# Five edits to the order of work in an attention and feed-forward kernel: a bank pair exchanged, a sum and an add issued in earlier steps, eight bias matmuls in place of five unread ones, one load ahead of another, values behind two products

## The chip, the cores and the metric

The kernel runs on one core of a Trainium2 chip. The core has five engines that run side by side, each through its own instructions in order: TensorE (matmuls; PE in the profile, and PEld for its weight loads), VectorE (DVE), ScalarE (ACT), GpSimd (POOL) and SyncE (SP). They wait for one another through semaphores. POOL and SP here issue most of the transfers (DMA) between the core's memory and the chip's main memory. TensorE writes only into PSUM, an accumulator memory of eight banks; VectorE and ScalarE read results out of them.

The metric is the device time of one execution, in microseconds (us), lower is better. All times below are in us unless they are marked ns, and positions are counted from the start of the profiled span.

## The reference

```python
scores = (q @ k^T) / sqrt(64)                          # 8 batches, 8 heads, 576 tokens
mask = (rel >= 0) & (rel < 128)                        # rel = query position - key position
attn = softmax(where(mask, scores - slope[h] * |rel|, -1e9))
x = (attn @ v), heads side by side                     # 4608 tokens x 512
h = x @ w_in                                           # 512 x 2048
g = where(h > 0, h, exp(min(h, 0)) - 1)
out = g @ w_out                                        # 2048 x 512, float32
```

Each query looks at itself and at the 127 keys before it, with a bias that falls linearly with the distance at a slope of its head.

## The kernel before, in words

**Attention.** A batch `b` has 576 tokens, in five blocks of 128 (the last has 64). For each block `u` of keys, scores are formed for the queries that can see it, ScalarE takes exponentials (`early_expo`, `first_expo`, `expo`) into `EX[u]`, and VectorE multiplies them with a table of bias and mask (`first_weigh`, `weigh`, L216 and L241). Batch 0 adds bias and mask on TensorE instead: matmuls with scaled identities (`early_bias`, L183, and `bias`, L166) write into the bank, and scores are added to them (`early_scores`, L191, and `first_scores`, L176). `values` (L253, a quarter of the banks) and `all_values` (L271, all heads into the bank pair `spa`, batches 2 to 7) then multiply with v, and a column of ones gives the softmax's denominator: VectorE takes a reciprocal and multiplies with it (L259 and L260, or L276 and L277). The result `xn` is turned into `xT` by `turn`: on TensorE with a copy (batches 0 and 1) or by a transfer that SP's queue issues (L285).

**Loads of q, k and v** are issued by POOL. Batches 0 and 1 come in pieces (`load_first`, L101), which TensorE transposes (`turn_first`, L136); later ones come by `load_qk` (L108) and VectorE turns them (`turn_qk`, L145). `load_v` is L114.

**Feed-forward.** `hidden` (L305) multiplies `xT` with w_in into `hp[0]`, `hp[1]` (some early blocks into others), ScalarE and POOL or ScalarE alone prepare the exponential, and `elu` (VectorE, L323) writes `g`. For most tokens the product with w_out isn't made directly but in the form with seven products of half size for a pair of 128-token blocks: pair `n` takes four sums of `g` blocks on VectorE (`sums`, S1 to S4, L354), seven products of eight matmuls each (`product`, L393), and adds that put the output together (`combine`: C11, C12, C22, also L354). Only the first two blocks of 128 tokens use the direct form (`output`, L329). Products of a pair go into two banks, `z` and `x`, chosen by the table `XY`: products 1, 6, 7 and 4 into `z`, products 2, 5 and 3 into `x`. ScalarE copies products 1, 6, 7 and 5 out (`kept`, L396). C11 adds the copy of product 1 to product 2, which lies in `x`; product 5 is the next to overwrite `x`.

**The order of work** is written by hand. After a start-up part (to L495) the loop at L674 goes through numbered steps `s`. In a step, these are emitted one after the other: `early` entries, the step's `hidden`, the `elu` of the step before, the `tasks` (entries by `at`, and by `at_once`, which puts them first), the `OUT` list (seven single product matmuls in most steps), and the `late` entries (by `after`). An engine runs its share in just this order, so an entry's place decides what stands ahead of it in each queue.

The steps concerned: the start-up has `warm(5, sp[0])` (L492), matmuls that nobody reads. Step 1 forms the second half of block 1's scores in `AB`, which is `spa`. In steps 11 and 12 POOL issues the third pieces of batch 1's k and q, in step 17 they are transposed. Steps 18 to 23 have no `hidden`; they begin batch 1's attention and the first pair (n = 1, steps 19 to 30). Before, its products 1, 6, 7, 4 go to `op` and 2, 5, 3 to `sp[3]`; the direct output of step 18 uses `op` too. `all_values(b, u)` comes in step `START[b] + 4 * u + 3`.

Of the kernel before, what the change touches and what calls it, by code (L numbers as in the profile page):

```python
# [18 lines left out]
def kernel(  # L19
# [57 lines left out]
    sp = [spa[:, 0, :], spa[:, 1, :]] + [ps_s.tile([128, 512], F32, name=f"sp{i}", tag=f"sp{i}") for i in (2, 3)]  # L77
    hp = [ps_h.tile([128, 512], F32, name=f"hp{i}", tag=f"hp{i}") for i in range(2)]
    av = ps_v.tile([128, 512], F32, name="av", tag="av")
    op = ps_o.tile([128, 512], F32, name="op", tag="op")  # L80
    AB = sp[0:2]
# [67 lines left out]
    with tc.manual_schedule():  # L149
# [29 lines left out]
        def early_bias(banks, c0):  # L179

            for x in range(4):
                for hh in range(2):
                    nc.tensor.matmul(banks[hh][:, 128 * x:128 * x + 128], SI[:, 4 * hh + x, :], RB[:, c0:c0 + 128],  # L183
                                     start=x == 0, stop=False, skip_group_check=True)
# [58 lines left out]
        def values(b, i, part, bank=av):  # L243

            m = 128 if i < 4 else 64
            banks = (part, part + 2) if b < 2 else (2 * part, 2 * part + 1)
            parts = [(3, 128, 3), (3, 192, 4)] if i == 4 else [(i, 0, i)] + ([(i - 1, 128, i - 1)] if i else [])
            a = bank[:, 0:4 * (D + 1)].rearrange("p (x h d) -> p x h d", x=2, h=2)
            for x, g in enumerate(banks):
                for h2 in range(2):  # L250
                    for j, (u, c, n) in enumerate(parts):
                        c += 512 * g + 256 * h2
                        nc.tensor.matmul(a[:, x, h2, :], ex_[u][:, c:c + 128], VP[b % 2][:, n, 2 * g + h2, 0:D + 1],  # L253
                                         start=j == 0, stop=j == len(parts) - 1)
            if part == 0:
                xnt[b, i] = work.tile([128, 4, 2, D], F16, name="xn", tag="xn", bufs=4)
            o = xnt[b, i][0:m, part::2, :, :] if b < 2 else xnt[b, i][0:m, 2 * part:2 * part + 2, :, :]
            r = work.tile([128, 2, 2], F32, name="rden", tag="rden", bufs=2)
            V.reciprocal(out=r[0:m], in_=a[0:m, :, :, D])  # L259
            V.tensor_tensor(out=o, in0=a[0:m, :, :, 0:D], in1=r[0:m].unsqueeze(3).broadcast_to([m, 2, 2, D]),  # L260
                            op=ALU.mult)
# [18 lines left out]
        def turn(b, i, copy=None, bank=op):  # L280
            n = 128 if i < 4 else 64
            o = (b * S + 128 * i) % RING
            x = xnt.pop((b, i)).rearrange("p g h d -> p (g h d)")
            if copy is None:
                nc.sync.dma_start_transpose(out=xT[:, :, o:o + n], in_=x[0:n, :])  # L285
                return
            t = bank.bitcast(F16)[:, 0:512].rearrange("p (c r) -> p c r", c=4)
            for c in range(4):
                nc.tensor.transpose(t[:, c, 0:n], x[0:n, 128 * c:128 * c + 128], ident[0:n, 0:n])
            copy(xT[:, :, o:o + n], t[:, :, 0:n])  # L290
# [80 lines left out]
        def place(n, i):  # L371


            z, x = XY[n] if n < 2 * NTB - 1 else (sp[2], sp[3] if i == 2 else sp[0])
            return (z if i in (1, 4, 6, 7) else x)[:, 0:256]
# [53 lines left out]
        def warm(n, bank=op):  # L429
            for _ in range(n):  # L430
                nc.tensor.matmul(bank[:, 0:256], wz[:, 0:128], wz, start=True, stop=True)
# [57 lines left out]
        early_expo((hp[1], av), 1, 0)  # L489
        values(0, 0, 0, hp[0])  # L490
        values(0, 0, 1, op)
        warm(5, sp[0])  # L492
        turn(0, 0, V.tensor_copy, hp[0])
        values(0, 1, 0)
        values(0, 1, 1, op)  # L495


        early, tasks, late, HID, OUT = {}, {}, {}, {}, {}

        def at(s, f, *a):  # L500
            tasks.setdefault(s, []).append((f, a))

        def at_once(s, f, *a):
            tasks.setdefault(s, []).insert(0, (f, a))

        def after(s, f, *a):
            late.setdefault(s, []).append((f, a))

        def before(s, f, *a):
            early.setdefault(s, []).append((f, a))  # L510
# [14 lines left out]
                HID[16 * t + 6 + j] = [(t, *step, BUF[(j + 1) % 2])]  # L525
        SEVEN = range(1, 18)

        XY = {1: (op, sp[3]), 2: (op, av)}
        for n in range(3, 2 * NTB):
            XY[n] = XY[n - 1][::-1]  # L530
        for o in range(16 * NTB):
            t, ts, f = o // 16, o // 4 % 4, o % 4
            if o // 8 in SEVEN:
                continue
            s = (9, 11, 13, 14)[o] if o < 4 else 11 + o if o < 13 else 2 * o - 1 if o < 16 else 15 + o
            OUT[s] = [(output, (t, ts, 4 * f, op if ts else sp[0]))]

        def done(r):
            for step in HID[r]:
                elu(*step)  # L540
# [2 lines left out]
        at(0, turn, 0, 1, V.tensor_copy)  # L543
        at(0, turn_first, 0, 0, 1, 0, sp[3], nc.scalar.copy)
        before(1, done, 0)
        at(1, early_bias, AB, 128)
        at(1, early_scores, AB, 1, 128)
        at(1, early_expo, AB, 1, 128)
        at(1, turn_first, 0, 1, 1, 0, av, V.tensor_copy)
# [28 lines left out]
        at(5, load_first, 1, 1, 0)  # L578
        at(9, load_first, 1, 0, 0)
        at(11, load_first, 1, 1, 1)  # L580
        at(12, load_first, 1, 0, 1)
        for n, s in enumerate((10, 11, 13, 14, 15)):
            at(s, load_v, 1, n)
        at(16, turn_first, 1, 1, 0, 0, av, V.tensor_copy)
# [5 lines left out]
        for u, a in ((0, 18), (1, 20)):  # L590
            for half in range(2):
                after(a, first_scores, 1, u, half, 2 * half)
                after(a, first_expo, 1, u, half, 2 * half, 0, 256)
                at(a + 1 + half, first_weigh, 1, u, half)
                if (u, half) != (1, 0):
                    after(a + 2 + half, values, 1, u, half, av if half else sp[2])
        after(22, turn, 1, 0, nc.scalar.copy, av)
# [19 lines left out]
        for b in range(2, B):  # L617
            for u in range(4):
                a = START[b] + 4 * u
                after(a, scores, b, u)  # L620
                for g in range(4):
                    before(a + 1 + g // 2, expo, b, u, g)
                at(a + 1, weigh, b, u, 0)
                at(a + 2, weigh, b, u, 1)
                at(a + 3, all_values, b, u)
                at(a + 3, turn, b, u)
                if u == 3:
                    at(a + 4, values, b, 4, 0, sp[2])
                    at(a + 4, values, b, 4, 1, sp[3])
                    at(a + 4, turn, b, 4)  # L630
            a = START[b - 1] if b > 2 else 0
            for n in range(4):
                piece = (b, int(n < 2), n % 2)
                if b == 2:
                    m = 4 if n < 2 else 6
                    at(TURN[b][n], turn_qk, *piece, 0, m)
                    at(REST[n], turn_qk, *piece, m, R)
                else:
                    at(TURN[b][n] if b == 3 else a + 4 * n, turn_qk, *piece)
            for n in range(8):  # L640
                at(a - 8 + n if a else 16 + n // 2, load_qk, b, int(n < 4), n % 4)
            for n in range(5):
                at(a + 3 + n if a else 20 + n // 2, load_v, b, n)
# [5 lines left out]
        for n in SEVEN:  # L649
            s = 15 + 8 * n  # L650
            ps = (19, 20, 21, 22, 23, 25, 27, 29, 30) if n == 1 else range(s, s + 9)
            if n < 2 * NTB - 1:
                for d, i in ((-1, 1), (1, 2), (3, 3), (4, 4)):
                    (at_once if n > 2 or n == 1 and i == 2 else at)(ps[d] if d > 0 else ps[0] - 1, sums, n, i)
                after(ps[2], combine, n, "C11")
                after(ps[6], combine, n, "C12")
                (at_once if n > 2 else at)(ps[8], combine, n, "C22")
                for d in range(8):
                    OUT[ps[d]] = [(product, (n, i, j, j + 1)) for i, j in turns[7 * d:7 * d + 7]]
            else:  # L660
                at_once(s - 3, sums, n, 3)
                for i in (2, 1):
                    at_once(s - 2, sums, n, i, 0, 6)
                    at_once(s - 1, sums, n, i, 6, 8)
                at(s - 1, product, n, 1)
                OUT[s] = [(product, (n, 2)), (combine, (n, "C11")), (sums, (n, 4)), (product, (n, 6)), (product, (n, 5))]
                OUT[s + 1] = [(product, (n, 7)), (product, (n, 3)), (combine, (n, "C22")), (combine, (n, "C12")),
                              (last_out, (n,))]
# [5 lines left out]
        for s in range(min(slots), max(slots) + 1):  # L674
            for f, a in early.get(s, []):
                f(*a)
            for step in HID.get(s, []):
                hidden(*step, s in SOFT)
            if s - 1 in HID and s not in (1, 4, 5):
                done(s - 1)  # L680
            for f, a in tasks.get(s, []):
                f(*a)
            for f, a in OUT.get(s, []):
                f(*a)
            for f, a in late.get(s, []):
                f(*a)
# [30 lines left out]
```

## Time and profile before

| | |
|---|---|
| median of 3 runs | 309.42 (308.7 to 309.49) |
| the profiled execution | 309.05 |
| its span, first to last instruction | 307.2 |
| TensorE clock granted | 1.0 |
| TensorE / VectorE / ScalarE / POOL busy | 97% / 84% / 79% / 35% of the span |
| matmuls of `hidden` (L305) | 144.2 busy |
| loads through POOL's queue | 18.36 MB |

A line of a timeline gives start, duration, engine, line, operation, what is written and read, sizes and count; brackets hold idle time of the engine just before it and what ended that. A line of waits gives who waited for whom: total, times, longest. The chain goes back from the last instruction, at each step to what released it. Names come without buffer numbers (`sp` for `sp[2]` and `sp[3]`, `s` for the staging of q and k in batches 0 and 1, `st` for later ones). Idle time of an engine that nobody waits for costs nothing.

### The profile page before, as it was taken

To read this page: it belongs to the slowest core of one execution; us is meant where nothing else is said; L and a number is where in the kernel's file an instruction comes from. 1 tells how busy PE (TensorE), PEld (TensorE's weight loads), DVE (VectorE), ACT (ScalarE), POOL (GpSimd) and SP (SyncE) were. 2 spreads that over 40 slices of the span, in tenths; PEclk is the share of its full clock that TensorE was granted. 3 is DMA by queue.
4 is the path that set the end of the run, shared out by engine and by line. 5 is a ranking of instruction groups with operands and counts; after the bars stand their busy time and mean duration, and the time that the engine had idled before them with its cause. 6 is when DMAs were issued, how large, how long until landed. Compare 5 with 4: busy or idle time off the path is not lost.

```text
span 307.2 us, 9841 instructions
## 1 busy us (share of the span) xinstructions
PE 299.3 (97%) x4079; PEld 256.6 (84%) x4079; DVE 257.6 (84%) x499; ACT 241.5 (79%) x445; POOL 108.8 (35%) x163
## 2 busy tenths in 40 slices
PE   7999998999999999999999999999999999999996
PEld 5788875898888888988888888888899888888885
DVE  5647878988989999997989998989998788886783
ACT  5576787769797798878888889778988797968881
POOL 8947848572343224141615061706000001010000
PEclk9999999999999999999999999999999999999999
DMA  9999999999395919294959995999730302230103
GB/s 97 174 200 199 202 183 193 113 123 110 33 154 74 170 27 170 37 163 42 134 68 139 111 106 76 138 127 116 64 97 3 95 17 88 19 97 1 73 16 121
DMA packets 96941, 32.04 MB, mean 104 GB/s; under 512 B 83968, under 2 KB 92800, under 8 KB 96896
## 3 DMA queue, kind: packets, MB, share of 16 engines
q0 software_dynamic: 75920, 18.36, 65.2%
q1 hardware_dynamic: 20832, 12.98, 18.2%
q8 instruction: 32, 0.52, 0.7%
q14 instruction: 13, 0.11, 0.1%
q10 hardware_dynamic: 144, 0.07, 0.1%
HBM read 36.70 MB, written 9.44 MB: 150 GB/s over the span
## 4 chain that ended last, share of the span: by engine, by line
PE 77%; DMA 6%; ACT 5%; DVE 5%; POOL 3%; issue 2%; POOLq 0%; DVEq 0%; ACTq 0%
PE hp L305 35%; PE op L393 13%; PE av L393 13%; PE spa L225 4%; DMA s<-in_q_dram 3%; PE spa L271 3%; DMA wi<-in_moe_w_in_dram 2%; PE sp L393 2%; DVE g L323 2%; ACT e L315 2%; PE sp L253 1%; ACT EX L236 1%; POOL e L316 1%; POOL VP L114 1%; PE sp L305 1%
## 5 line engine op out<-in xcount | busy, mean ns | idle before, releaser
L305 PE MATMUL hp<-xT,wi 128*128 128x256 f16 (+3 forms) x1488 | 144.2, 245 | 1.0 <-DVE g L323 0.5
L305 PEld LDWEIGHTS <-wi 128*128 128x128 f16 x1600 | 119.7, 98 | 18.2 <-issue 5.8
L323 DVE SCALAR_TENSOR_TENSOR g<-e,hp 128x512 f16<-128x512 f32 x138 | 93.6, 679 | 22.4 <-ACT e L313 12.7
L316 POOL TENSOR_SCALAR e<-e 128x512 f32<-128x512 f32 x44 | 28.4, 645 | 154.6 <-ACT e L315 151.3
L312 ACT ACTIVATE e<-hp 128x512 f32<-128x512 f32 x98 | 58.6, 598 | 28.8 <-PE hp L305 23.2
L313 ACT ACTIVATE e<-e 128x512 f32<-128x512 f32 x100 | 63.1, 631 | 3.2
L393 PEld LDWEIGHTS <-S 128*128 128x128 f16 x544 | 51.4, 98 | 7.5 <-issue 1.8
L393 PEld LDWEIGHTS <-g 128*128 128x128 f16 x400 | 37.5, 98 | 4.5 <-issue 0.4
L241 DVE TENSOR_TENSOR EX<-EX,TAB 128x1024 f16<-128x1024 f16 x48 | 32.9, 686 | 6.1 <-ACT EX L236 4.0
L114 POOL DMA_DIRECT2D VP<-in_v_dram x40 | 34.3, 867 | 3.0 <-DMA s<-in_k_dram 1.8
L315 ACT ACTIVATE e<-hp 128x512 f32<-128x512 f32 x40 | 24.0, 601 | 10.6 <-PE hp L305 10.6
L393 PE MATMUL op<-T,S 128*128 128x256 f16 x200 | 30.0, 273 | 0.0
L233 ACT ACTIVATE EX<-spa 128x1024 f16<-128x1024 f32 x24 | 24.6, 1026 | 3.7 <-PE spa L225 3.4
L393 PE MATMUL av<-T,S 128*128 128x256 f16 x176 | 26.4, 272 | 0.1
L236 ACT ACTIVATE EX<-sp 128x512 f16<-128x512 f32 x48 | 26.0, 597 | 0.0
L354 DVE TENSOR_TENSOR S<-g 128x1024 f16<-128x1024 f16 (+2 forms) x35 | 23.5, 671 | 0.7 <-PE op L393 0.2
L393 PE MATMUL op<-wo,g 128*128 128x256 f16 x128 | 19.0, 272 | 0.1
L393 PE MATMUL av<-wo,g 128*128 128x256 f16 x120 | 18.0, 273 | 0.0
L108 POOL DMA_DIRECT2D st<-in_k_dram x24 | 16.3, 688 | 3.1 <-DMA s<-in_q_dram 1.9
L277 DVE TENSOR_TENSOR xn<-spa,rden 128x512 f16<-128x512 f32 x24 | 16.6, 692 | 0.8
L108 POOL DMA_DIRECT2D st<-in_q_dram x24 | 15.9, 668 | 0.6 <-DMA VP<-in_v_dram 0.4
L271 PE MATMUL spa<-VP,EX 128*128 128x65 f16 x336 | 15.5, 193 | 0.1
(139 smaller groups left out, 380.3 us busy)
## 6 DMA issues: line engine op xcount, KB each, us to landing
out_dram<-ob SPq DMA_DIRECT2D x32, 256.0 KB, 3.1
VP<-in_v_dram POOLq DMA_DIRECT2D x32, 128.0 KB, 6.0
st<-in_k_dram POOLq DMA_DIRECT2D x24, 144.0 KB, 5.6
st<-in_q_dram POOLq DMA_DIRECT2D x24, 144.0 KB, 6.1
wi<-in_moe_w_in_dram POOLq DMA_DIRECT2D x4, 512.0 KB, 11.4
wo<-in_moe_w_out_dram POOLq DMA_DIRECT2D x4, 512.0 KB, 11.8
out_dram<-ob SPq DMA_DIRECT2D x7, 128.0 KB, 1.7
VP<-in_v_dram POOLq DMA_DIRECT2D x8, 64.0 KB, 6.1
```

Of the source, the lines that this page charges most:

```text
L108: nc.gpsimd.dma_start(st[b][32 * g:32 * g + 32, w, :, :, :, :].rearrange("p h n j d -> p (h n) (j d)"), (q, k)[w][b, 2 * g:2 * g + 2, :, : ...
L114: nc.gpsimd.dma_start(VP[b % 2][0:p, n, :, 0:D], v[b, :, 128 * n:128 * n + p, :].rearrange("h p d -> p h d"))
L236: nc.scalar.activation(unit(b, u)[:, g, :, :], sp[g].rearrange("p (h c) -> p h c", h=2), AF.Exp, scale=0.125)
L241: V.tensor_tensor(out=e, in0=e, in1=TAB[:, int(u == 3), 2 * gp:2 * gp + 2, :, :], op=ALU.mult)
L271: nc.tensor.matmul(a[:, h // 4, h % 4, :], ex_[u][:, c:c + 128], VP[b % 2][:, n, h, 0:D + 1], start=j == 0, stop=j == len(parts) - 1)
L305: nc.tensor.matmul(p[:, l * w + u0:l * w + u1], w_in_sb[:, c, fc * 128:(fc + 1) * 128], xT[:, c, x0:x0 + u1 - u0], start=(c == 0), stop=(c ...
L312: nc.scalar.activation(e[:, 0:n], p[:, 0:n], AF.Relu, scale=-1.0)
L313: nc.scalar.activation(e[:, 0:n], e[:, 0:n], AF.Exp, scale=-1.0)
L315: nc.scalar.activation(e[:, 0:n], p[:, 0:n], AF.Exp)
L316: nc.gpsimd.tensor_scalar(out=e[:, 0:n], in0=e[:, 0:n], scalar1=1.0, scalar2=0.0, op0=ALU.min, op1=ALU.max)
L323: V.scalar_tensor_tensor(out=gs[t][:, f0:f0 + nf, c0:c0 + w], in0=sh(es.pop((t, c0, f0))), scalar=1.0, in1=sh(hps.pop((t, c0, f0))), op0=A ...
L393: nc.tensor.matmul(o, a[:, j, :], b[:, j, :], start=j == 0 and i in (1, 2, 5), stop=j == 7, skip_group_check=True)
```

## The change

1. The five unread matmuls of the start-up go, and the eight bias matmuls of step 1 (`early_bias(AB, 128)`) are issued in their place.
2. The third piece of q for batch 1 is loaded in step 11, ahead of a piece of v, not in step 12.
3. In pair 1 the two banks are exchanged: products 1, 6, 7, 4 go to `sp[3]`, and 2, 5, 3 to `op`.
4. In pair 1, S3 is formed in step 18 (was 22), C11 comes right behind the last matmul of product 2 in step 21 (was at that step's end, behind `values(1, 0, 1)`), and the weighing of block 1's first half moves from step 21 to step 22.
5. `all_values` and `turn` of batches 2 to 7 are emitted behind the first two product matmuls of their step, not ahead of them. By the same edit they come behind all of the step's `tasks`; in step 34 that puts `sums(2, 3)` ahead of them on VectorE.

```diff
         values(0, 0, 1, op)
-        warm(5, sp[0])
+        early_bias(AB, 128)
         turn(0, 0, V.tensor_copy, hp[0])
...
+        def amid(s, f, *a):
+            mid.setdefault(s, []).append((f, a))
...
-        XY = {1: (op, sp[3]), 2: (op, av)}
+        XY = {1: (sp[3], op), 2: (op, av)}
...
-        at(1, early_bias, AB, 128)
...
-        at(12, load_first, 1, 0, 1)
+        at(11, load_first, 1, 0, 1)
...
-                at(a + 1 + half, first_weigh, 1, u, half)
+                at(22 if u else a + 1 + half, first_weigh, 1, u, half)
...
-                at(a + 3, all_values, b, u)
-                at(a + 3, turn, b, u)
+                amid(a + 3, all_values, b, u)
+                amid(a + 3, turn, b, u)
...
-                for d, i in ((-1, 1), (1, 2), (3, 3), (4, 4)):
+                for d, i in ((-1, 1), (1, 2), (3 if n > 1 else -1, 3), (4, 4)):
                     (at_once if n > 2 or n == 1 and i == 2 else at)(ps[d] if d > 0 else ps[0] - 1, sums, n, i)
-                after(ps[2], combine, n, "C11")
+                if n > 1:
+                    after(ps[2], combine, n, "C11")
...
+                if n == 1:
+                    OUT[ps[2]].insert(2, (combine, (n, "C11")))
...
-            for f, a in OUT.get(s, []):
+            for n, (f, a) in enumerate(OUT.get(s, [])):
+                if n == 2:
+                    for g, b in mid.pop(s, []):
+                        g(*b)
+                f(*a)
+            for f, a in mid.get(s, []):
                 f(*a)
```

More of the change, by code (lines that the diff above doesn't have):

```diff
@@ L495 @@
         values(0, 1, 1, op)
-        early, tasks, late, HID, OUT = {}, {}, {}, {}, {}
+        early, tasks, mid, late, HID, OUT = {}, {}, {}, {}, {}, {}
         def at(s, f, *a):
```

## The prediction

> **What bounds the kernel now.** I read the page first. TensorE is busy for 97% of the span, VectorE and ScalarE for 84% and 79%:
>
> ```profile
> PE 299.3 (97%) x4079; PEld 256.6 (84%) x4079; DVE 257.6 (84%) x499; ACT 241.5 (79%) x445; POOL 108.8 (35%) x163
> ```
>
> So time comes only from TensorE work taken off its queue, or from the few places where TensorE stands still. The view of waits, for TensorE alone, lists those (total, times, longest):
>
> ```profile
> PE sp L393 <- DVE ob L354: 1.2, 1, 1.2
> PE hp L305 <- DVE g L323: 0.5, 3, 0.2
> ...
> PE sp L136 <- DMA s<-in_q_dram: 0.2, 1, 0.2
> ```
>
> The first is by far the longest wait after the start. The chain that ended last (start, us, what) shows what comes ahead of it:
>
> ```profile
> 33.62 0.71 POOL s L101
> 34.34 0.84 POOL VP L114
> 35.17 10.50 DMA s<-in_q_dram
> 45.67 0.04 issue
> 45.72 0.31 PE sp L136 x8
> 46.03 1.85 PE op L329 x8
> 47.88 0.02 issue
> 47.90 0.60 ACT ob L336
> 48.50 0.04 issue
> 48.54 1.03 PE op L393 x8
> ```
>
> All before 45.72 is on the chain only through one 64 KB load of q, issued behind a v load. VectorE's timeline up to the long wait (start, us):
>
> ```profile
> 49.45 0.69 DVE L216 TENSOR_TENSOR EX<-EX,TAB 128x1024 f16<-128x1024 f16 x1 [1.15 <-ACT EX L205]
> ...
> 51.92 0.69 DVE L216 TENSOR_TENSOR EX<-EX,TAB 128x1024 f16<-128x1024 f16 x1
> 52.52 0.18 DVE L259 RECIPROCAL rden<-av 128x4 f32<-128x4 f32 x1
> 52.74 0.42 DVE L260 TENSOR_TENSOR xn<-av,rden 128x256 f16<-128x256 f32 x1
> 53.08 0.41 DVE L354 TENSOR_TENSOR ob<-U,sp 128x256 f32<-128x256 f32 x1
> ```
>
> The add that empties the bank (C11, 53.08) stands behind a weighing and a normalisation; product 5, which overwrites that bank, starts at 53.54, though TensorE had issued the matmul before it at 52.09. And the start, from the timeline:
>
> ```profile
> 15.43 0.61 PE L183 MATMUL spa<-T 128*128 128x128 f16 x8
> ...
> 17.58 0.95 DVE L140 COPY QT<-hp 128x768 f16<-128x768 f16 x1
> ```
>
> **What the Trainium skill says.** "PSUM — Partial Sum Buffer", section "Engine vs sequencer instructions": ScalarE's and VectorE's queues are strict FIFO, and matmuls start and complete in program order. The trace agrees: VectorE's C11 had its inputs by 51.4 and ran at 53.08, after what was written ahead of it. "DMA: Bandwidth & Descriptors", section "Queues, rings and completion order": a DMA engine consumes a ring's descriptors in order. Here landings follow issues: k at 33.62 landed at 44.05, v at 34.30 at 45.26, q at 35.17 at 45.67. "TensorE: Matmul & The Clock Gate", section "Wait — 56ns, not 53.3ns?": 55.6 ns per warm matmul of 128 columns; the trace has 56 to 57.
>
> **Part by part.**
>
> *Biases early.* Five unread matmuls (109 ns each, 0.55) at 10.19 give way to eight biases (8 x 0.056 = 0.45). TensorE waits there for VectorE until 10.96, and for w_in's landing (12.61) until 12.66, so this costs nothing; without that cover it still would be 0.1 less work. In step 1 the same eight go: 0.45 off TensorE at 15.43. What is late next? The exponential at 16.41 can start at 16.23, where ScalarE gets free, and its end frees the bank pair for step 2's biases 0.18 sooner (17.48 to 17.30). VectorE's copies of k and q, which waited for TensorE, move by the full 0.44, so q's copy ends at 18.09 and no longer binds. The biases take 0.76 to their last start and 0.20 to the next kind: scores at 18.27 against 18.59, a gain of **0.32**. It must pass w_out's first landing (29.10; the matmul reading it is at 29.49, then 29.17): just free.
>
> *q's third piece.* In step 11 it goes ahead of v's piece, on POOL's queue at 34.30 instead of 35.17. In ring order it follows k's landing by its own 0.41 (45.67 - 45.26): 44.46. TensorE wants it at 45.31 - 0.32 = 44.99. So the whole stall goes: the step from 45.28 to 45.72 is 0.44 where its neighbours take 0.03, **0.41**. The v piece passed over lands by 45.67, is read at 54.6: free. Bounds: 0, and all 0.32 above lost too, if the landing stays at 45.67; 0.41 at best.
>
> *Banks exchanged.* Product 1 no longer waits for ScalarE's copy of op (47.90 to 48.50): TensorE goes from scores to product in 0.20 instead of 0.40. But the first values then wait for the weighing that ended at 50.14 (values at 50.20); ScalarE's order behind that is unchanged. I count **0**; bounds 0 and 0.1.
>
> *C11 and S3.* New VectorE order from the weighing at 49.45, in the old clock: sum S2, weighing, reciprocal, normalisation to 51.89, then C11, 51.81 to 52.22. Product 6 ends its issue at 52.20, so product 5 starts at 52.28: 53.54 - 52.28 = 1.26. Behind C11 come the other normalisation (to 52.78, wanted by the transposes, which lose 0.12), then two weighings of 0.61 a start: the first ends at 53.44, values(1,1,0) want it at 53.48. Net **1.14**. S3 (0.65) goes from 54.37 to 48.2, inside VectorE's 1.15 idle; were that cover gone it would push the weighing at 49.45, and TensorE with it, by up to 0.65. Lower bound: 0.5, if the moved weighing lands a full instruction late. Upper 1.3.
>
> *Values behind two products.* Two matmuls are 0.22. VectorE's reciprocal behind the values never sits idle before its 24 runs, and comes 0.32 or more after the values' last matmul, so starting these 0.22 later is covered; without cover each of 24 costs up to 0.22. Gain: in 8 of 24 places the values themselves wait for a weighing, 0.09 to 0.27. Those at 75.2, 144.3 and 244.2 run into a later wait (C11, g, g) and give nothing; those at 109.3 (0.20), 117.0 (0.12), 132.7 (0.16), 211.0 (0.22 of 0.27) and 226.4 (0.11) give 0.8 at most; VectorE trails there, so I take **0.3**, bounds -0.3 and 0.8. For n=2 the sum S3 now comes before reciprocal and normalisation (0.9): product 7 no longer waits at 78.24, **0.1**. The transpose by SP's queue goes 0.68 later; it landed at 80.01 and is read at 82.57.
>
> Sum: 0.32 + 0.41 + 0 + 1.14 + 0.3 + 0.1 = 2.3. The profiled execution took 309.05 (span 307.2 and 1.85 around it), 0.37 under the median of the three runs: 306.75 against the one, 307.1 against the other. I say **307.0**.
>
> Does the gain live until the end? From 54 on engines and POOL's loads follow TensorE's steps, so all should move together. The exception is the transposes through SP: TensorE waited 0.31 for one at 98.34 (landed 98.29), and those landing at 114.36 and 129.90 are read at 114.43 and 130.15.
>
> ```profile
> L305 PE MATMUL hp<-xT,wi x248: 192/247/283, 90.3 to 134.9; 128*128 128x256 f16 x60, 128*128 128x192 f16 x32, 128*128 128x64 f16 x32
> ...
>   DMA xT<-xn: 0.3, 1
> ```
>
> **Rivals.**
> 1. *The q piece still lands at 45.67.* For: its load is 10.5 from issue to landing in a full queue. Against: landings follow issues. Loses 0.73: 307.7.
> 2. *The wait moves from C11 to the weighings behind it.* For: the margin is 0.04 in my working. Against: S3 is gone from that stretch. If C11's gain shrinks to 0.5 and the values' part gives nothing: 308.0.
> 3. *Landings of transposes don't follow.* If the one at 98.29 keeps its time, the 2.0 gained by then goes into the wait, and 0.3 remains: 308.8, no change.
> 4. *Slower.* A transpose took 2.3 to 7.3 from issue to landing, depending on what loads run beside it. The one at 111.94 took 2.4, with 0.07 to spare; shifted against the loads to 7.3 it stalls TensorE by 4.8, and 2.3 - 4.8 = +2.5: 311.9. It decides once such stalls pass 3.2 in all (the gain of 2.3, and 0.93, which is 0.3%). Against: loads are issued behind POOL's minimum instructions, which follow TensorE.
>
> That the change doesn't do as said: C11 would have to stay last on VectorE; the diff puts it ahead of the values' instructions, so I give it nothing apart.
>
> **Chances.** About 0.3%, here 0.93, is what a measurement of this kernel can tell from no change. Main forecast 0.60 (306.3 to 307.8); rival 1 0.14, rival 2 0.10, rival 3 0.07, rival 4 0.09. Faster takes main, rival 1 and 0.07 of rival 2: 0.81. Same takes the other 0.03 and rival 3: 0.10. Slower is rival 4: 0.09. The range runs from 306.2 (values' part at its upper bound) to 308.8 (rival 3), leaving out rival 4 and tails.
>
> **What would show it.** Right: scores near 18.27; no DMA wait near 45; C11 before the values' reciprocal, and product 5 within 0.3 of product 6; S3 near 47.5; TensorE 1.8 ahead at 57, 2.3 at the end. Wrong: values(1,1,0) or the transposes before them waiting over 0.3 for VectorE (rival 2); a longer DMA wait at the matmuls reading xT (rivals 3, 4); q's landing after 45 (rival 1).

## The result, and the profile after

The changed kernel took a median of 307.0 (306.44 to 308.26) against 309.21 (308.7 to 309.51) for the kernel before on the same chip, six runs each: a ratio of 0.9932 with a 95% interval of 0.9911 to 0.9953. The profiled execution took 307.11, with a span of 305.2 (before: 309.05 and 307.2). The forecast of 307.0 was met; whether for its reasons is the question of what follows.

Busy times of the engines, from the page of the changed kernel:

```profile
PE 297.6 (98%) x4074; PEld 255.7 (84%) x4074; DVE 257.8 (84%) x499; ACT 241.2 (79%) x445; POOL 109.1 (36%) x163
```

Five matmuls fewer, as the diff says; what the kernel won is mostly time in which TensorE stood still. The view of waits for TensorE, same kernel:

```profile
PE hp L136 <- DMA s<-in_q_dram: 1.1, 1, 1.1
PE hp L305 <- DVE g L323: 0.8, 4, 0.3
...
PE av L393 <- DVE ob L354: 0.3, 1, 0.3
```

The 1.2 for C11 (`ob`, L354) and the wait for q's piece near 45 (0.2) are gone. The largest of those shown is now 1.1 for a load at the very start, where the execution of before waited 0.3; no edit touches that load. The chain that ended last, in the stretch shown of before:

```profile
45.23 0.45 PE av L136 x16
45.68 0.37 PE sp L136 x16
46.05 1.85 PE op L329 x8
```

In this stretch no DMA is on it any more: the transposes of q's third piece (`sp` L136, x16) follow the ones before them directly. VectorE's timeline in the stretch of the old wait:

```profile
48.06 1.29 DVE L354 TENSOR_TENSOR S<-g 128x1024 f16<-128x1024 f16 x2
...
51.82 0.41 DVE L354 TENSOR_TENSOR ob<-U,op 128x256 f32<-128x256 f32 x1
52.15 0.18 DVE L259 RECIPROCAL rden<-av 128x4 f32<-128x4 f32 x1
...
52.70 1.28 DVE L216 TENSOR_TENSOR EX<-EX,TAB 128x1024 f16<-128x1024 f16 x2
```

C11 (51.82) stands ahead of the second reciprocal, S3 is one of the two sums in the 1.29 at 48.06, and the two weighings (52.70) come behind both normalisations. TensorE in the same stretch:

```profile
51.88 0.49 PE L393 MATMUL sp<-T,S 128*128 128x256 f16 x3
52.29 0.60 PE L393 MATMUL op<-T,S 128*128 128x256 f16 x4
```

Product 5 (`op`, 52.29) follows product 6 without a gap.

**How the gain is counted below.** The start of an execution varies by more than most of these edits are worth, so two absolute times can't be compared. I use three marks on ScalarE instead, its first operation on certain hidden tiles: A, of step 17, the last before pair 1; B, the next one, behind pair 1's long stretch; C, the last of all. From ScalarE's timeline of before:

```profile
44.25 0.60 ACT L312 ACTIVATE e<-hp 128x512 f32<-128x512 f32 x1 [0.76 <-PE hp L305]
...
56.97 0.60 ACT L315 ACTIVATE e<-hp 128x512 f32<-128x512 f32 x1 [0.80 <-PE hp L305]
```

and of after:

```profile
44.70 0.60 ACT L312 ACTIVATE e<-hp 128x512 f32<-128x512 f32 x1 [0.76 <-PE hp L305]
...
55.83 0.60 ACT L315 ACTIVATE e<-hp 128x512 f32<-128x512 f32 x1 [0.80 <-PE hp L305]
```

C starts at 296.75 and 294.80. A to B took 12.72 before and 11.13 after (1.59 won); B to C took 239.78 and 238.97 (0.81 won). Up to A the changed kernel was 0.45 late in this pair of executions, so 1.59 + 0.81 - 0.45 = 1.95 of the spans' difference of 2.0 is placed. For the start I use a fourth stretch, from the first matmul of step 1's hidden (L305) to block 2's first scores (L176). How far the marks repeat can be read from kernels that do the same work: without a wait for q and with the old pair 1, A to B is 12.27 to 12.31 in four kernels, so differences of some hundredths count there. B to C is looser. Where the work behind B is that of before it took 239.78 (before), 239.94, 239.68 and 239.57 (experiments 1, 9 and 10), and most of that spread comes at one place near 98, a wait for a transposed `xT`. Gains behind B are therefore read place by place.

### The profile page after: what moved, and what is told of

Its sections match the earlier page's. It is cut to its first block, busy times and chain, and to the rows that moved or that the text cites. A ratio compares the mean times of both kernels' runs of the same rounds, so it can differ in the third digit from the quotient of the medians.

```text
span 305.2 us, 9832 instructions
## 1 busy us (share of the span) xinstructions
PE 297.6 (98%) x4074; PEld 255.7 (84%) x4074; DVE 257.8 (84%) x499; ACT 241.2 (79%) x445; POOL 109.1 (36%) x163
## 4 chain that ended last, share of the span: by engine, by line
PE 76%; DVE 7%; ACT 7%; DMA 4%; issue 3%; POOL 1%; POOLq 0%; DVEq 0%; ACTq 0%
PE hp L305 34%; PE op L393 13%; PE av L393 12%; PE spa L225 3%; PE spa L271 3%; DVE g L323 2%; DMA VP<-in_v_dram 2%; DMA s<-in_q_dram 2%; ACT EX L236 2%; PE sp L305 2%; PE sp L393 1%; ACT e L315 1%; PE op L329 1%; POOL e L316 1%; PE spa L329 1%
## 5 line engine op out<-in xcount | busy, mean ns | idle before, releaser
L305 PE MATMUL hp<-xT,wi 128*128 128x256 f16 (+3 forms) x1488 | 144.2, 245 | 1.1 <-DVE g L323 0.8
L305 PEld LDWEIGHTS <-wi 128*128 128x128 f16 x1600 | 119.7, 98 | 18.4 <-issue 6.6
L393 PE MATMUL av<-T,S 128*128 128x256 f16 x176 | 27.2, 272 | 0.3 <-DVE ob L354 0.3
L354 DVE TENSOR_TENSOR S<-g 128x1024 f16<-128x1024 f16 (+2 forms) x35 | 23.4, 672 | 0.8 <-PE op L393 0.2
L393 PE MATMUL op<-wo,g 128*128 128x256 f16 x128 | 19.7, 273 | 0.0
L225 PE MATMUL sp<-QT,KT 32*128 32x256 f16 (+2 forms) x240 | 15.1, 250 | 0.0
```

What stands on the lines that cost most here:

```text
L305: nc.tensor.matmul(p[:, l * w + u0:l * w + u1], w_in_sb[:, c, fc * 128:(fc + 1) * 128], xT[:, c, x0:x0 + u1 - u0], start=(c == 0), stop=(c ...
L393: nc.tensor.matmul(o, a[:, j, :], b[:, j, :], start=j == 0 and i in (1, 2, 5), stop=j == 7, skip_group_check=True)
```

## The experiments

My theory is the sum on record. The rivals to be told apart: that the start's two edits are swallowed or hide one another; that C11 alone makes the gain and the exchange, the sum and the weighing are ornament; or that they are its cover; and that the values' edit is worth nothing. Each experiment names the kernel that its diff starts from. Where a run gave one time only, that time is told, and the reading is from the marks.

**1. Edits 1 and 2 alone** (biases, q's third piece; from before).

```diff
-        warm(5, sp[0])
+        early_bias(AB, 128)
...
-        at(1, early_bias, AB, 128)
...
-        at(12, load_first, 1, 0, 1)
+        at(11, load_first, 1, 0, 1)
```

> The first two edits alone (biases in place of the unread matmuls, q's third piece in step 11). Theory A, gains that add up: the step of scores of block 2 comes 0.43 sooner after the first hidden matmuls, no wait for q's third piece, so 0.85 less at step 18 if q's first load lands as it did in the profile of before (7.0), and the less the later that load lands: 0 if it lands at 7.9, as it did in the profile of the changed kernel. Total 0 to 0.8 faster than before. Theory B, the biases themselves delay the start (TensorE's clock or the bank pair): q's first load lands at 7.0 again and the first hidden matmul is still 0.6 later than in before.

Median 309.12 of 14 runs against 309.37; ratio 0.9997, interval 0.9984 to 1.001. By the marks both edits do as forecast: the matmuls reading q's piece run without a wait, A to B is 12.27 against 12.72, and the start's stretch is 3.62 against 4.04. TensorE's timeline at the start, before:

```profile
14.54 1.05 PE L305 MATMUL hp<-xT,wi 128*128 128x128 f16 x16
...
18.58 0.40 PE L176 MATMUL spa<-QT,KT 64*128 64x256 f16 x4
```

and with these two edits:

```profile
14.67 1.05 PE L305 MATMUL hp<-xT,wi 128*128 128x128 f16 x16
...
18.29 0.39 PE L176 MATMUL spa<-QT,KT 64*128 64x256 f16 x4
```

From step 1's hidden to block 2's scores it is 0.42 less. Yet the most that the interval allows, 0.5 (309.37 x 0.0016), is less than the 0.42 + 0.45 that the marks show. So in the times part of this gain isn't there. Experiment 3 shows one way in which it is lost.

**2. Edits 3 and 4 alone** (banks, C11, S3, weighing; from before).

```diff
-        XY = {1: (op, sp[3]), 2: (op, av)}
+        XY = {1: (sp[3], op), 2: (op, av)}
...
-                at(a + 1 + half, first_weigh, 1, u, half)
+                at(22 if u else a + 1 + half, first_weigh, 1, u, half)
...
-                for d, i in ((-1, 1), (1, 2), (3, 3), (4, 4)):
+                for d, i in ((-1, 1), (1, 2), (3 if n > 1 else -1, 3), (4, 4)):
...
-                after(ps[2], combine, n, "C11")
+                if n > 1:
+                    after(ps[2], combine, n, "C11")
...
+                if n == 1:
+                    OUT[ps[2]].insert(2, (combine, (n, "C11")))
```

> The edits to pair 1 alone (banks exchanged, S3 in step 18, C11 behind product 2, the weighing in step 22). Theory A: product 5 starts within 0.1 of product 6's end instead of 1.4 behind it; 1.1 to 1.2 faster than before from step 24 on, and in the end. Rival: the wait comes back at the weighings behind C11 or in later steps; 0.5 or less in the end.

Median 308.18 of 22 runs; ratio 0.9967, interval 0.9954 to 0.998. Its profiled execution began late, so only intervals are read. A came 2.21 later than in before: 1.30 of it by the first load of q (landed at 8.30, before 7.00), the rest behind a stretch from 9.22 to 12.63 in which TensorE was granted half its clock, with matmuls of 128 columns 0.107 apart instead of 0.056. A to B is 11.13, exactly that of the whole change, though q's piece wasn't moved here. With a late start the piece (landed at 45.32) is there when it is wanted. The comparison for the C11 part is therefore a kernel in which no wait for q is left either, experiment 1: 12.27 - 11.13 = 1.14. B to C is 239.69, 0.09 less than before. It is won between 98 and 101, where TensorE's wait for a transposed xT is that much shorter (0.22, before 0.31). That is no gain of these edits: kernels with the work of before there waited 0.47 (experiment 1), 0.22 (experiment 9) and less than 0.1 (experiment 10).

**3. Edit 5 alone** (values behind two products; from before).

```diff
...
-                at(a + 3, all_values, b, u)
-                at(a + 3, turn, b, u)
+                amid(a + 3, all_values, b, u)
+                amid(a + 3, turn, b, u)
...
-            for f, a in OUT.get(s, []):
+            for n, (f, a) in enumerate(OUT.get(s, [])):
+                if n == 2:
+                    for g, b in mid.pop(s, []):
+                        g(*b)
+                f(*a)
+            for f, a in mid.get(s, []):
                 f(*a)
```

> The last edit alone (values behind two products). Theory A: the eight waits of the values for a weighing go, five of them for good, 0.7 to 0.9 faster in the end. As predicted: 0.3 to 0.4 (the rest comes back as waits for VectorE). Rival: VectorE gets its input late, hidden matmuls wait longer for g, no gain or slower.

Median 308.38 of 9 runs against 309.37; ratio 0.9984, interval 0.9964 to 1.0005. The medians are further apart than this ratio says, and one of the nine times, 311.04, lies far above the rest; but the interval includes 1, so by the times alone a gain isn't shown. The marks show it. B to C is 239.07, 0.71 less than before, where I had allowed 0.4. Following the marks of single steps against before: 0.12 won by step 34's sum S3 (forecast 0.1), nothing at 109.3, 0.14 at 117, 0.17 at 132.7, 0.22 at 211 and 0.12 at 226. That is the list of the forecast less its first entry. At 109.3 the values no longer wait (they start at 109.42, 0.22 behind the first of the two products), but the next hidden matmuls then wait for `g`, as at 144.3 and 244.2, which I had struck out.

The same run bears on experiment 1's puzzle. It was 0.47 late at step 17 against before (why, is told in the last section), yet only 0.04 late at B, without any edit near there (TensorE's timeline):

```profile
45.63 0.44 PE L136 MATMUL sp<-ident,s 64*64 64x64 f16 x16
46.00 1.25 PE L329 MATMUL op<-wo,g 128*128 128x512 f16 x5
```

The piece of q had landed at 45.12, and TensorE, late by 0.47, found it there. A to B is 12.29, the length without a wait. In before, where the piece landed at 45.67, a start later by up to some 0.45 would have cost nothing either: the old wait for q swallows it. With the piece loaded sooner nothing swallows a late start, and edit 2 gains the less the later the execution begins. It also depends on the landing: 45.12 would have been soon enough even for the start of before, whose TensorE wanted the piece at 45.28. Of the four profiled executions that load it in step 12 (before, experiments 2, 3 and 9) only that of before waits for it.

**4. The whole change again**, beside experiments 1 to 3 on their chip.

> The changed kernel once more. Theory A: from step 24 on it is ahead of before by 1.14 and by 2.0 over the whole stretch after step 18, as in its first profile; its start depends on when q's first load lands (7.0 to 7.9), so the time in all is 306.3 to 307.3. Theory B: the start is late again by 0.5 to 0.9, with q's first load at 7.0.

Median 306.8 (306.22 to 307.16) of 6 runs; ratio 0.992, interval 0.9907 to 0.9933. A to B 11.13, B to C 238.97: both as in the first profile of the change, to 0.01. In these two executions everything behind A repeats, and what differs lies ahead of it.

**5. Banks as before, all else changed** (from after).

```diff
-        XY = {1: (sp[3], op), 2: (op, av)}
+        XY = {1: (op, sp[3]), 2: (op, av)}
```

> The whole change but for the exchange of banks: pair 1 has products 1, 6, 7, 4 in op again. As predicted, the exchange is worth 0 to 0.1: product 1 starts 0.2 later behind ScalarE's copy of op, and the first values of batch 1 start when they did, at the weighing's end; step 18 to step 24 takes the 11.13 of the changed kernel, at most 0.1 more. Rival, that the exchange carries part of the gain at C11: 0.2 to 0.4 more.

One time, 307.71. A to B is 11.14. TensorE's timeline of this kernel, which runs 0.77 later than after's:

```profile
49.33 1.03 PE L393 MATMUL op<-wo,g 128*128 128x256 f16 x8
...
50.98 0.30 PE L253 MATMUL sp<-VP,EX 128*128 128x65 f16 x4
```

and of after:

```profile
48.35 1.05 PE L393 MATMUL sp<-wo,g 128*128 128x256 f16 x8
...
50.21 0.30 PE L253 MATMUL sp<-VP,EX 128*128 128x65 f16 x4 [0.15 <-DVE EX L216]
```

Product 1 is issued 0.98 sooner with the exchange, of which 0.77 is the start; but the values are 0.77 sooner and no more, since they then wait for their weighing: the exchange moves a wait and is worth 0.01.

**6. The weighing where it was** (from after).

```diff
-                at(22 if u else a + 1 + half, first_weigh, 1, u, half)
+                at(a + 1 + half, first_weigh, 1, u, half)
```

> The whole change, but the weighing of block 1's first half is in step 21 again, ahead of C11 on VectorE. If C11's place in VectorE's queue is what counts: C11 waits for that weighing, which can't start before ScalarE's exponential ends; product 5 starts 0.7 later than in the changed kernel, and step 18 to step 24 takes 0.6 to 0.7 more (11.8). Rival, that C11's own place in the step's list does it all: no more than 0.1 more.

One time, 307.68; A to B 11.85, so 0.72 of the C11 part is gone. VectorE's timeline of this kernel:

```profile
51.96 0.69 DVE L216 TENSOR_TENSOR EX<-EX,TAB 128x1024 f16<-128x1024 f16 x1
52.57 0.41 DVE L354 TENSOR_TENSOR ob<-U,op 128x256 f32<-128x256 f32 x1
```

and its TensorE:

```profile
53.04 0.60 PE L393 MATMUL op<-T,S 128*128 128x256 f16 x4 [0.63 <-DVE ob L354]
```

One weighing (0.61 from start to start) stands ahead of C11 again, and product 5 waits 0.63 for it. This is what the Trainium skill says of VectorE's queue ("PSUM — Partial Sum Buffer", "Engine vs sequencer instructions": strict FIFO), with its price in this place.

**7. S3 where it was** (from after).

```diff
-                for d, i in ((-1, 1), (1, 2), (3 if n > 1 else -1, 3), (4, 4)):
+                for d, i in ((-1, 1), (1, 2), (3, 3), (4, 4)):
```

> The whole change, but S3 of pair 1 is formed in step 22 again, behind two weighings and a transpose. If the idle time of VectorE in step 18 is a cover that matters: product 7 waits for S3 by 0.7 to 0.8, and step 18 to step 24 takes 0.6 to 0.8 more (11.8). Rival, S3 was never late: 11.1.

One time, 307.41; A to B 11.94, so 0.81 is gone, of which 0.21 comes back in the first steps behind B (B to C 238.74). VectorE's timeline of this kernel:

```profile
54.08 0.65 DVE L354 TENSOR_TENSOR S<-g 128x1024 f16<-128x1024 f16 x1
```

and its TensorE:

```profile
54.79 0.50 PE L393 MATMUL sp<-T,S 128*128 128x256 f16 x3 [0.64 <-DVE S L354]
```

With C11 sooner, the next thing late is S3 itself, which product 7 needs and which stands behind two weighings and a transpose. So with only one of its two companions C11's early place keeps 0.42 (experiment 6) or 0.33 (here) of its 1.14.

**8. An attempt at more: a transpose of later q and k in another step** (from after). In the whole change (experiment 4's execution) TensorE waits 0.26 at 74.88 for an add of VectorE (`ob`, 74.44), directly behind a transpose of k (`turn_qk`, 74.01); this edit puts that transpose into a later step.

```diff
-        REST = 32, 33, 36, 37
+        REST = 32, 35, 36, 37
```

> The whole change, and the second part of batch 2's k transposes on VectorE (512 ns) goes from step 33 to step 35, so that C11 of pair 2 and the elu behind it come 0.5 sooner. Theory: the wait of product 5 of pair 2 for C11 (0.4) and of the next hidden matmul (0.16) go: 0.4 to 0.55 less after step 33, 306.4 in all. Rival: VectorE is that much late in step 35, and the next hidden matmuls wait: no gain.

Ratio 0.9923, interval 0.9908 to 0.9937, median 306.94: no better than after's second measurement (0.992). From VectorE's timeline of this kernel:

```profile
77.19 1.16 DVE L145 STREAM_TRANSPOSE KT<-st 128x320 int32<-128x320 int32 x2
78.28 0.65 DVE L354 TENSOR_TENSOR S<-g,S 128x1024 f16<-128x1024 f16 x1
78.85 0.68 DVE L323 SCALAR_TENSOR_TENSOR g<-e,hp 128x512 f16<-128x512 f32 x1
```

Against experiment 4, whose steps just ahead agree with it to 0.01, the hidden matmuls at 77.61 are 0.18 sooner (there 77.79), and those at 79.58 are 0.12 later (there 79.46). What is won is lost again, since VectorE now has two transposes in a row (1.16) ahead of the `g` that the second needs. B to C is 239.17, 0.20 longer. The rival expectation held.

**9. Edit 1 alone, and 10. edit 2 alone** (from before; each is its half of experiment 1's diff), to see each without the other.

> The biases moved alone, q's third piece still in step 12. Theory: TensorE is 0.3 to 0.45 sooner at step 2 for the same landings at the start, and gives all of it back to the wait for q's third piece: by step 24 no sooner than before (56.97 if that piece lands at 45.67). Rival, the gain at the start is kept: 0.3 sooner at step 24. The landing of q's first load is 7.0 or 7.9 as chance has it, though pair 1 isn't touched.

> q's third piece sooner, alone. Theory: step 17 to step 24 takes 12.27 to 12.29 instead of 12.72, whatever the start, as the load lands ahead of its use. Rival, the piece of v that it passes is late in its place: some other wait in steps 17 to 24 and 12.5 or more.

Edit 1 alone took 309.44, one time. The view of waits for TensorE shows why that says little:

```profile
PE hp L305 <- DMA wi<-in_moe_w_in_dram: 0.9, 1, 0.9
```

The first piece of w_in landed at 13.31 (before: 12.61), which put the first hidden matmuls 0.69 later than before. So whether the q wait gives the biases' gain back stays untested in this form; A to B was 12.31, without a wait for q, as in experiment 3 (the piece landed at 46.26 and TensorE read it from 46.30). Edit 2 alone took 308.43, one time. Its start was that of before within 0.03 (step 1's hidden at 14.56 against 14.54, scores at 18.61 against 18.58), so it is the clean measurement of the q wait: A to B 12.28 against 12.72, a gain of 0.44. Its transposes of q's piece run at 45.18 with no wait ahead of them.

**11. The first load of q ahead of POOL's table** (from after), against the start's 1.1.

```diff
-        nc.gpsimd.iota(rel, pattern=[[1, 256]], base=0, channel_multiplier=-1)
         load_first(0, 0, 0)
+        nc.gpsimd.iota(rel, pattern=[[1, 256]], base=0, channel_multiplier=-1)
```

> The whole change, and POOL issues the first load of q ahead of the 0.37 iota instead of behind it. Theory, now that nothing later hides the start: q's first load lands up to 0.4 sooner and the whole kernel ends 0.2 to 0.4 sooner, 306.5. Rival, that load waits for the data of k's first load in the DMA engines and not for its issue: it lands as before, and the identity that k's transposes need comes 0.7 later; same or up to 0.3 slower.

Ratio 0.9913, interval 0.9888 to 0.9938, median 306.73: the same as after. In the profiled execution q landed at 6.92 (after: 7.89), but w_in's first piece landed at 13.52 (after: 12.24), and TensorE waited 0.79 for that one. Its scores of block 2 came at 18.99, after's at 19.04.

## Why the prediction was right, point by point

- **Biases early, forecast 0.32, measured 0.42** (3.62 against 4.04; also 3.62 in after and in experiments 4, 6, 8 and 11). Where later pieces of q or k landed late, the gain is smaller or gone: 3.80 in experiment 7, 3.83 in experiment 9, 4.33 in experiment 5. The term was mis-sized by 0.10. I let the exponential start at 16.23, a full duration (0.60) behind ScalarE's operation before it; in experiment 1 it started 0.49 behind that (15.76, then 16.25). The Trainium skill ("ScalarE: Activation LUTs", "What ACT_TABLE_LOAD costs") says that back-to-back operations overlap by some 93 ns; the 0.11 here agrees, and I had not used it. Putting the biases in place of the unread matmuls cost nothing, as forecast: from the first scores to step 1's hidden it takes 6.31 in after (9.11 to 15.42) and 6.31 in experiment 3 (8.70 to 15.01), which has the unread matmuls.
- **q's third piece, forecast 0.41, measured 0.44** (experiment 10). The forecast of ring order held: after's piece landed at 44.13, ahead of v's at 44.84, and in every profile the pieces of q, k and v issued around it landed in their order of issue. What the working missed is that this wait is also a cover: in before it swallows a late start. So this edit gains 0.44 only where the start is as early, and the piece as late, as in the profiled execution of before. Experiment 1's interval (a gain of at most 0.50) fits 0.42 for the biases and little for q; which starts the unprofiled executions had is not shown.
- **Banks exchanged, forecast 0, measured 0.01** (experiment 5), by the mechanism named: the wait moves to the values behind the weighing.
- **C11 and S3, forecast 1.14, measured 1.14** (experiments 1 and 2). Experiments 6 and 7 show that the two moves that I had counted only as its cover are worth 0.72 and 0.81 (0.6 by the end): each, left out, puts another wait of 0.63 or 0.64 on TensorE's path, at product 5 or at product 7. They don't add up, since each is needed for the whole. C11 left at its step's end with the other two moved was not run.
- **Values behind two products, forecast 0.3, measured about 0.58**, the largest miss. I had named the eight places rightly but paid the five open ones at less than half, "VectorE trails there". In four of the five it doesn't: they stood on the list with 0.61 and paid 0.65, of which 0.07 was lost again between them. Only 109.3 behaved as the discount assumed. The failed step is to scale a sum when it should have been decided place by place, as it had been for 75.2, 144.3 and 244.2.
- **S3 of n = 2, forecast 0.1, measured 0.12.**
- **Not on the list:** in after some 0.1 less wait for a transposed xT near 98, the place where rival 3 expected a loss. It varies by more than that among executions with the same work (experiment 2), so I don't count it as won by the change.
- **The sum.** 0.42 + 0.44 + 0.01 + 1.14 + 0.58 + 0.12 = 2.71 against 2.3. The medians moved by 2.2 and by 2.57. So two errors met: the edits were worth 0.4 more than I said, and executions with a late start lose up to 0.44 of it, because q's wait no longer hides them. That 307.0 was met to the hundredth is partly luck. In the pair of profiles it can be seen directly: TensorE was 1.14 ahead at B and 1.95 at the end, where I had written 1.8 and 2.3: the start had made it 0.45 late at A, in spite of the biases. For the same reason the scores that I had put near 18.27 came at 19.04: q's first load landed 0.88 later than in before. Whether the start is late by chance or goes with the kernel isn't settled (last section).
- **The rivals.** 1 (q's piece still late) fell with its landing at 44.13. 2 (the wait moves to the weighings behind C11) did not happen with all three moves; the nearest to it is experiment 7, where it moves to S3 behind two weighings. 3 and 4 (transposes land late) did not occur in any profile of the whole change: the matmuls that read xT waited no more than 0.2 for one in after, against 0.31 in before. In experiment 1, whose work there is that of before, one was 0.47.

What stays open: what makes the first loads of q and w_in land where they do, and TensorE's full clock come when it does. Their spread (below) decides more than half a microsecond of each execution, and in experiment 11 issuing one of them sooner didn't win it.

## What to carry to other kernels

When an instruction is moved ahead on an engine that serves in order, ask at once for the next late thing and for the one after: here the early add keeps 0.33 or 0.42 of its 1.14 if the sum or the weighing stays where it was. A wait for a load is a cover for everything that is late ahead of it, so removing it gains only what the start leaves, and the start's spread then shows in the result. And where the start of an execution varies, measure an edit between two marks that hold the same work, instead of in the median of the whole.

## What the runs showed of the hardware that I had not expected

- **The first loads land differently from profile to profile.** With the same order of issue, q's first piece landed between 6.89 and 8.30 in the profiled executions of before, after and experiments 1 to 10, and w_in's first piece between 11.94 and 13.37. They did not move together: experiment 2 had the latest q (8.30) with w_in at 12.28, experiment 5 q at 7.94 with the latest w_in. Whether that is chance or goes with the kernel is open: the five kernels without edits 3 and 4 had q at 6.89 to 7.03, the six with them at 7.12 to 8.30, and the one kernel profiled twice at 7.89 and 7.70. If it goes with the kernel, the medians hold a price of the change that the list above doesn't name. Part of it varies between executions of one kernel: six times of the changed kernel on one chip (experiment 4) spread from 306.22 to 307.16.
- **The start also hangs on when TensorE gets its full clock.** In the profiled executions it was granted in full from some point between 4.34 (before) and 6.88 (experiment 3). In the start-up's unread matmuls of 256 columns the two rates can be seen: in experiment 3 they start 0.213 apart to the end, in before the last ones 0.109 apart. Experiment 3's execution reached the first scores 0.48 later than before (8.70 and 8.22), though q's first piece landed at 6.94 (before: 7.00) and was not waited for: its late start is that of the slower matmuls. In experiment 2's execution the clock went back to half for 3.41, behind a wait of 1.16 for q's first load; the five of its 22 executions with a mean granted clock of 0.994 took 309.29 to 309.55, the others 307.24 to 308.81. What brings this about isn't shown: after waited 1.1 for the same load and kept the full clock.
- **What follows repeats closely, but for one wait.** From mark A on, the two profiled executions of the changed kernel agree to 0.01 over 250 us, and kernels that share an edit agree in its stretch to some hundredths (A to B without q's wait and with the old pair: 12.27, 12.28, 12.29, 12.31). The exception is the wait for a transposed xT near 98, between less than 0.1 and 0.47 in kernels with the same work there.
